# Nyström attention with a Silu feed-forward: an in-kernel list scheduler orders all engines, with DMA transposes, scores on 64x32 parts, Ln/Exp denominators, GpSimd sums and Silu

## The chip, the cores and the metric

The kernel runs on one core of one Trainium2 chip. The metric is the device time of one execution in microseconds (us), the slowest core's. Each run of a kernel is marked fast or slow. Here, with one core, slow only means more than 1.5% above the fastest run of the same kernel. PE is TensorE, PEld its weight load, DVE VectorE, ACT ScalarE, POOL GpSimd, SP SyncE.

## The reference

Eight batches of eight heads, 576 tokens of 64; then two layers on all 4608 tokens (d_model 512, d_ff 2048):

```python
q_lm = q.reshape(B, H, 32, S // 32, D).mean(axis=3)      # landmarks; k_lm the same
A, Bm, C = sm(q, k_lm), sm(q_lm, k_lm), sm(q_lm, k)      # sm: scaled scores, softmax
Z = Bm.T / (norm1(Bm) * norminf(Bm) + 1e-06)
for _ in range(6):
    Z = 2 * Z - Z @ Bm @ Z                               # Newton-Schulz
x = A @ Z @ C @ v                                        # then heads merged
h = x @ w_in
out = (h * sigmoid(h)) @ w_out
```

The kernels never form x: they make m = (Z C v) w_in for each batch, and the first layer is A times m.

## The kernel before

Its order is made by hand. The attention of batch b+1 is a generator with 26 stops. Its steps are dealt out evenly between whole units of the two layers of batch b:

```python
    def l1_unit(b, dc):
        h_ps = big("h_ps")
        for g in range(NG):
            for hf in range(2):
                mm(h_ps[:, hf, 0:HS2], m_t[b][:, g, dc * 128:(dc + 1) * 128],
                   etn_t[b][:, g, hf * HS2:(hf + 1) * HS2], start=(g == 0), stop=(g == 1))
        sig = sgp.tile([128, 2, HS2], BF, tag="sig", name="sig")
        nc.scalar.activation(out=sig, in_=h_ps[:, :, 0:HS2], func=AF.Tanh, scale=0.5)
        o = (b % 2) * S
        nc.vector.scalar_tensor_tensor(          # (tanh + 1) * h, halved in the last copy
            out=gT[:, dc, o:o + S].rearrange("p (f x) -> p f x", f=2), in0=sig, scalar=1.0,
            in1=h_ps[:, :, 0:HS2], op0=OP.add, op1=OP.mult)
    # ... cut ...
        gen = attn(b + 1) if b + 1 < B else iter(())
        NST = 26
        done = 0
        for i, u in enumerate(units):            # units: first and second layer of b
            want = (i + 1) * NST // len(units)
            while done < want:
                done += 1
                next(gen, None)
            u()
```

Transposes of q and k are VectorE's (32x32 blocks), landmark sums TensorE's (matmuls with the identity), Exp and Tanh share one table set, so ScalarE loads a table once.

The softmax here doesn't subtract the row's maximum and nothing guards it: scores larger than these inputs give would overflow.

Of the kernel before, what the change touches and what calls it, by code (L numbers as in the profile page):

```python
# [11 lines left out]
AX = mybir.AxisListType  # L12


@with_exitstack
def kernel(
# [12 lines left out]
    J = S // L  # L29
    NTOK, DMODEL = out.shape  # L30
# [4 lines left out]
    VP = VA * L  # L35
    sc = 1.0 / float(Dh) ** 0.5
    HS2 = S // 2

    constp = ctx.enter_context(tc.tile_pool(name="constp", bufs=1))
    natp = ctx.enter_context(tc.tile_pool(name="natp", bufs=2))  # L40
    vp = ctx.enter_context(tc.tile_pool(name="vp", bufs=1))
    qtp = ctx.enter_context(tc.tile_pool(name="qtp", bufs=2))
    smp = ctx.enter_context(tc.tile_pool(name="smp", bufs=2))
    stp = ctx.enter_context(tc.tile_pool(name="stp", bufs=3))
    etp = ctx.enter_context(tc.tile_pool(name="etp", bufs=2))
    mp = ctx.enter_context(tc.tile_pool(name="mp", bufs=2))
    sgp = ctx.enter_context(tc.tile_pool(name="sgp", bufs=3))
    outp = ctx.enter_context(tc.tile_pool(name="outp", bufs=3))
    bigp = ctx.enter_context(tc.tile_pool(name="bigp", bufs=2, space=bass.MemoryType.PSUM))
    opsp = ctx.enter_context(tc.tile_pool(name="opsp", bufs=2, space=bass.MemoryType.PSUM))  # L50
    smps = ctx.enter_context(tc.tile_pool(name="smps", bufs=2, space=bass.MemoryType.PSUM))

    def big(nm):
        return bigp.tile([128, 2, 512], FP, tag="big", name=nm)

    def small(nm):
        return smps.tile([128, 512], FP, tag="small", name=nm)
# [5 lines left out]

    w_in_sb = constp.tile([128, 4, DFF], BF, tag="w_in_sb", name="w_in_sb")
    w_out_sb = constp.tile([128, NDC, DMODEL], BF, tag="w_out_sb", name="w_out_sb")
    NV = 2
    vslots = [vp.tile([VP, H, 2, VI * Dh], BF, tag=f"v{i}", name=f"v{i}") for i in range(NV)]
    qk_t = [None] * B

    def load_qk(b):  # L70
        qk = natp.tile([128, 2, NG, J, Dh], BF, tag="qk", name="qk")
        for t, src in ((1, k), (0, q)):
            nc.gpsimd.dma_start(  # L73
                out=qk[:, t].rearrange("p g j d -> p g (j d)"),
                in_=src[b].rearrange("(g h) (l j) d -> (h l) g (j d)", g=NG, l=L))
        qk_t[b] = qk

    def load_v(b):
        vs = vslots[b % NV]
        for a in range(VA):  # L80
            nc.gpsimd.dma_start(
                out=vs[a * L:(a + 1) * L, :, 0, :],
                in_=v[b].rearrange("h (l a x) d -> a l h (x d)", l=L, a=VA)[a])

    def load_w_in():

        for fc in range(4):
            if fc < 2:
                nc.gpsimd.dma_start(out=w_in_sb[:, fc, :],
                                    in_=moe_w_in[fc * 128:(fc + 1) * 128, :])  # L90
            else:
                for r in range(2):
                    nc.gpsimd.dma_start(
                        out=w_in_sb[64 * r:64 * r + 64, fc, :],
                        in_=moe_w_in[fc * 128 + 64 * (1 - r):fc * 128 + 64 * (2 - r), :])

    def load_w_out():
        for c in range(4):
            nc.gpsimd.dma_start(
                out=w_out_sb[:, 4 * c:4 * c + 4, :],  # L100
                in_=moe_w_out[c * 512:(c + 1) * 512, :].rearrange("(c p) n -> p c n", p=128))

    load_qk(0)


    idb = constp.tile([128, 128], BF, tag="idb", name="idb")
    nc.vector.memset(idb, 1.0)
    nc.gpsimd.affine_select(out=idb, in_=idb, compare_op=OP.is_equal, fill=0.0, base=0,
                            pattern=[[-1, 128]], channel_multiplier=1)
    hmask = constp.tile([128, 4, L], BF, tag="hmask", name="hmask")  # L110
    nc.vector.memset(hmask, 0.0)
    for a in range(4):
        nc.vector.memset(hmask[L * a:L * (a + 1), a, :], 1.0)
    honesb = constp.tile([128, 4], BF, tag="honesb", name="honesb")
    nc.vector.tensor_copy(out=honesb, in_=hmask[:, :, 0])

    selm = constp.tile([128, NG, 2, H], BF, tag="selm", name="selm")
    nc.vector.memset(selm, 0.0)
    for g in range(NG):
        for a in range(4):  # L120
            nc.vector.memset(selm[L * a:L * (a + 1), g, :, 4 * g + a:4 * g + a + 1], 1.0)
    sel = constp.tile([2 * H, NG, 128], BF, tag="sel", name="sel")
    for g in range(NG):
        sel_ps = smps.tile([128, 1024], BF, tag="small", name="sel_ps")
        nc.tensor.transpose(out=sel_ps[0:2 * H, 0:128],
                            in_=selm[:, g].rearrange("p t h -> p (t h)"), identity=idb)
        nc.vector.tensor_copy(out=sel[:, g, :], in_=sel_ps[0:2 * H, 0:128])  # L127
    for i in range(NV):
        nc.vector.memset(vslots[i][:, :, 1, :], 1.0)

    def bc(ap, n, axis):

        shape = list(ap.shape)
        shape.insert(axis, n)
        return ap.unsqueeze(axis).to_broadcast(shape)

    etn_t = [None] * B
    m_t = [None] * B


    def attn(b):
        qk = qk_t[b]
        vs = vslots[b % NV]


        lm_ps = small("lm_ps")
        lmv = lm_ps[:, 0:256].rearrange("p (t g d) -> p t g d", t=2, g=NG)
        if b == 0:
            for t in (1, 0):
                for j in range(J):  # L150
                    mm(lmv[:, t], idb, qk[:, t, :, j, :], start=(j == 0), stop=(j == J - 1))
                yield
        else:
            for j in range(J):
                mm(lmv, idb, qk[:, :, :, j, :], start=(j == 0), stop=(j == J - 1))
                if j == 8:
                    yield
        lm = smp.tile([128, 256], BF, tag="lm", name="lm")
        nc.scalar.copy(out=lm, in_=lm_ps[:, 0:256])  # L159

        qT = qtp.tile([128, 2, NG, 2, J, L], BF, tag="qT", name="qT")


        def tp(t, g):
            if t == 0:
                nc.vector.transpose(  # L166
                    out=qT[:, 0, g].rearrange("p c j l -> p j c l"),
                    in_=qk[:, 0, g].rearrange("p j (c x) -> p j c x", c=2))
            else:
                for c in range(2):  # L170
                    nc.vector.transpose(  # L171
                        out=qT[:, 1, g, c].rearrange("p (i a) l -> p a i l", a=VA),
                        in_=qk[:, 1, g].rearrange("p (a i) (c x) -> p a i c x", a=VA, c=2)[:, :, :, c])
# [7 lines left out]
        def LB(t, g, c):  # L181
            return lmbd[:, (t * NG + g) * 2 + c].rearrange("p a l -> p (a l)")
# [311 lines left out]
```

## Time and profile before

| | before |
|---|---|
| time | 315.28 us median of 2 runs (314.69 to 315.87) |
| span, mean granted clock | 312.8 us, 0.984 |
| busy: PE, DVE, ACT, POOL | 280.7 (90%), 207.4 (66%), 166.8 (53%), 32.0 us (10%) |
| packets under 512 bytes | 944 of 18379 |

### The profile page before, as it was taken

Reading aid. Unit: us, or ns where it says so; the run is one execution under the profiler, and the core shown is the slowest. Engines: PE = TensorE matmul, PEld = TensorE weight load, DVE = VectorE, ACT = ScalarE, POOL = GpSimd, SP = SyncE. Lnnn points to the kernel's source line nnn. Section 1 sums busy time; section 2 is a strip of 40 time slices with the busy share of each in tenths; the row PEclk is TensorE's granted clock in tenths of the full one; section 3 lists DMA queues with packets and bytes.
Section 4 is the critical chain, followed back from the end, with each engine's and each line's share of the span. In section 5 each row is a group of like instructions: output and inputs, shape, how many; then the busy total and the mean of one; then the engine's idle time right before and its main releaser. Section 6 shows DMA issues by size and latency. Waiting matters only on the chain.

```text
span 312.8 us, 5645 instructions
## 1 busy us (share of the span) xinstructions
PE 280.7 (90%) x2268; PEld 161.9 (52%) x2268; DVE 207.4 (66%) x420; ACT 166.8 (53%) x277; POOL 32.0 (10%) x55
## 2 busy tenths in 40 slices
PE   0465889979999999999999999999999999999990
PEld 0443464546555654666455744665465644555440
DVE  6857689998988697579747794676448664555000
ACT  1042664775466665765475646565645757555110
POOL 7342302100210020102001020000000000000000
PEclk9998699999999999999999999999999999999997
DMA  6999999672528152193418261110111101121122
GB/s 116 210 209 207 206 210 209 86 147 69 96 50 151 56 91 56 45 161 62 83 55 145 73 90 46 52 24 16 35 55 36 44 11 45 47 47 56 52 77 75
DMA packets 18379, 28.16 MB, mean 90 GB/s; under 512 B 944, under 2 KB 9136, under 8 KB 18352
## 3 DMA queue, kind: packets, MB, share of 16 engines
q0 software_dynamic: 13600, 18.35, 34.6%
q1 hardware_dynamic: 4752, 9.44, 10.8%
q8 instruction: 18, 0.29, 0.4%
q14 instruction: 9, 0.07, 0.1%
HBM read 36.70 MB, written 9.44 MB: 147 GB/s over the span
## 4 chain that ended last, share of the span: by engine, by line
PE 72%; DVE 11%; DMA 8%; ACT 4%; issue 2%; POOL 1%; POOLq 0%; ACTq 0%
PE ops L60 36%; PE h_ps L60 18%; DVE gT L393 5%; DMA v_97<-in_v_dram 4%; PE lm_ps L60 3%; DMA w_in_sb<-in_moe_w_in_dram 3%; PE m_ps L60 3%; PE c_ps L60 2%; ACT sig L391 2%; PE w_ps L60 2%; PE sa_ps L60 2%; PE ns_ps L60 2%; DVE qT L171 2%; PE rb_ps L60 1%; ACT m L377 1%
## 5 line engine op out<-in xcount | busy, mean ns | idle before, releaser
L60 PE MATMUL ops<-w_out_sb,gT 128*128 128x512 bf16 x576 | 150.6, 379 | 0.1
L393 DVE SCALAR_TENSOR_TENSOR gT<-sig,h_ps 128x576 bf16<-128x576 bf16 x128 | 94.8, 746 | 53.2 <-ACT sig L391 53.0
L391 ACT ACTIVATE sig<-h_ps 128x576 bf16<-128x576 f32 x128 | 82.4, 651 | 56.9 <-PE h_ps L60 54.4
L60 PE MATMUL h_ps<-etn,m 128*128 128x288 bf16 x512 | 84.3, 287 | 3.4 <-DVE gT L393 2.6
L60 PEld LDWEIGHTS <-gT 128*128 128x128 bf16 x576 | 52.5, 98 | 44.3 <-issue 6.3
L60 PEld LDWEIGHTS <-m 128*128 128x128 bf16 x512 | 47.9, 98 | 34.6 <-issue 11.6
L377 ACT CAST m<-m_ps 128x1024 bf16<-128x1024 f32 x32 | 32.1, 1019 | 14.2 <-PE m_ps L60 14.1
L409 ACT ACTIVATE ost<-ops 128x512 f32<-128x512 f32 x36 | 21.4, 598 | 21.8 <-PE ops L60 21.6
L60 PE MATMUL lm_ps<-qk,idb 128*128 128x256 bf16 (+1 forms) x162 | 22.2, 289 | 6.3 <-DVE sel L127 6.3
L171 DVE STREAM_TRANSPOSE qT<-qk 128x576 bf16<-128x576 bf16 x32 | 23.8, 755 | 1.6 <-PE c_ps L60 1.6
L239 DVE SCALAR_TENSOR_TENSOR st<-st,ns_ps 128x320 bf16<-128x320 bf16 (+1 forms) x48 | 20.7, 432 | 5.5 <-PE ns_ps L60 5.4
L60 PEld LDWEIGHTS <-idb 128*128 128x128 bf16 x162 | 16.2, 112 | 11.2 <-issue 6.8
L166 DVE STREAM_TRANSPOSE qT<-qk 128x1152 bf16<-128x1152 bf16 x16 | 21.7, 1354 | 0.0
L304 ACT ACTIVATE ct<-c_ps 96x768 bf16<-96x768 f32 x16 | 12.9, 806 | 7.5 <-PE c_ps L60 7.5
L60 PE MATMUL ns_ps<-st 128*128 128x160 bf16 (+1 forms) x96 | 13.7, 223 | 2.1 <-DVE st L239 1.4
L60 PE MATMUL m_ps<-w_in_sb,zt 64*32 64x512 bf16 x256 | 13.8, 414 | 1.8 <-ACT m L377 1.0
L60 PE MATMUL c_ps<-lmbd,qT 128*96 128x128 bf16 x192 | 14.2, 219 | 0.2 <-ACT et L256 0.2
L60 PEld LDWEIGHTS <-qT 128*96 128x96 bf16 x192 | 13.3, 123 | 1.9 <-issue 0.4
L159 ACT CAST lm<-lm_ps 128x256 bf16<-128x256 f32 x8 | 3.0, 375 | 20.3 <-PE lm_ps L60 20.3
L290 DVE TENSOR_TENSOR etn<-et,rb_ps 128x576 bf16<-128x576 bf16 x16 | 12.0, 748 | 1.9 <-PE rb_ps L60 1.8
L256 ACT ACTIVATE et<-sa_ps 128x576 bf16<-128x576 f32 x16 | 10.4, 648 | 3.9 <-PE sa_ps L60 3.8
L73 POOL DMA_DIRECT2D qk<-in_k_dram x8 | 5.8, 720 | 62.3 <-PE lm_ps L60 45.4
(78 smaller groups left out, 171.4 us busy)
## 6 DMA issues: line engine op xcount, KB each, us to landing
out_dram<-ost SPq DMA_DIRECT2D x32, 256.0 KB
qk<-in_k_dram POOLq DMA_DIRECT2D x8, 576.0 KB, 5.6
qk<-in_q_dram POOLq DMA_DIRECT2D x8, 576.0 KB, 8.9
v_96<-in_v_dram POOLq DMA_DIRECT2D x12, 192.0 KB, 6.4
v_97<-in_v_dram POOLq DMA_DIRECT2D x12, 192.0 KB, 6.6
w_out_sb<-in_moe_w_out_dram POOLq DMA_DIRECT2D x4, 512.0 KB, 16.1
w_in_sb<-in_moe_w_in_dram POOLq DMA_DIRECT2D x2, 512.0 KB, 11.1
w_in_sb<-in_moe_w_in_dram POOLq DMA_DIRECT2D x4, 256.0 KB, 12.2
```

The lines of the kernel that those rows point to most:

```text
L60: nc.tensor.matmul(out=out_ap, lhsT=lhsT, rhs=rhs, start=start, stop=stop, skip_group_check=True)
L73: nc.gpsimd.dma_start(out=qk[:, t].rearrange("p g j d -> p g (j d)"), in_=src[b].rearrange("(g h) (l j) d -> (h l) g (j d)", g=NG, l=L))
L166: nc.vector.transpose(out=qT[:, 0, g].rearrange("p c j l -> p j c l"), in_=qk[:, 0, g].rearrange("p j (c x) -> p j c x", c=2))
L171: nc.vector.transpose(out=qT[:, 1, g, c].rearrange("p (i a) l -> p a i l", a=VA), in_=qk[:, 1, g].rearrange("p (a i) (c x) -> p a i c x", ...
L239: nc.vector.scalar_tensor_tensor(out=st2[:, :, lo:SW], in0=st[:, :, lo:SW], scalar=2.0, in1=ns_ps[:, 0:NG * SW].rearrange("p (g x) -> p g ...
L256: nc.scalar.activation(out=et.rearrange("p (f x) -> p f x", f=2), in_=sa[:, :, 0:HS2], func=AF.Exp, scale=sc / J)
L290: nc.vector.tensor_tensor(out=etn[:, g, :].rearrange("p (f x) -> p f x", f=2), in0=ets[g].rearrange("p (f x) -> p f x", f=2), in1=rb[:, :, ...
L304: nc.scalar.activation(out=ct.rearrange("p (f x) y -> p f (x y)", f=2), in_=c_ps[0:VP, :, 0:384], func=AF.Exp, scale=sc / J)
L377: nc.scalar.copy(out=m_sb[:, :, f * 512:(f + 1) * 512], in_=m_ps)
L391: nc.scalar.activation(out=sig, in_=h_ps[:, :, 0:HS2], func=AF.Tanh, scale=0.5)
L393: nc.vector.scalar_tensor_tensor(out=gT[:, dc, o:o + S].rearrange("p (f x) -> p f x", f=2), in0=sig, scalar=1.0, in1=h_ps[:, :, 0:HS2], op ...
L409: nc.scalar.activation(out=ost, in_=ops, func=AF.Copy, scale=0.5)
```

## The change

Its intent: give TensorE less work (scores on 64x32 parts, denominators by a block of ones, landmark sums on GpSimd), take half of VectorE's work away (Silu on ScalarE, transposes by DMA), and let a list scheduler inside the kernel place every instruction of every engine, with the Exps of a batch in one group so that Exp and Silu need few table loads. The scheduler simulates the engines with assumed durations and delays and emits the order that it finds; on the chip each engine then runs its list in order, with semaphore waits for data alone. The diff, cut to its core:

```diff
+class Plan:
+    LAG = {"PE": 0.25, "ACT": 0.22, "DVE": 0.12, "POOL": 0.2, "SP": 2.0}   # us to the next engine
+    MARGIN = 0.15                                                         # PE only
+    def run(self):
+        # ... cut: at each event each idle engine takes its ready candidate of lowest prio ...
+def act_us(n): return 0.165 + 0.000835 * n
+def dve_us(n): return 0.146 + 0.00104 * n
+def mm_us(n, count=1): return count * max(n / 2400 + 0.0025, 0.028)
 # ... cut ...
-    bigp = ctx.enter_context(tc.tile_pool(name="bigp", bufs=2, space=bass.MemoryType.PSUM))
-    opsp = ctx.enter_context(tc.tile_pool(name="opsp", bufs=2, space=bass.MemoryType.PSUM))
-    smps = ctx.enter_context(tc.tile_pool(name="smps", bufs=2, space=bass.MemoryType.PSUM))
+    pairs = [psp.tile([128, 2, 512], FP, tag=f"ps{i}", name=f"ps{i}") for i in range(4)]
+    def bank(o):
+        i = o.slot[0]
+        return pairs[i // 2][:, i % 2, :]
 # ... cut: per batch; TensorE does transposes and sums itself for the first NPE = 2 batches ...
-                nc.vector.transpose(out=qT[:, 0, g]..., in_=qk[:, 0, g]...)
+                        lambda e, t=t, g=g: nc.sync.dma_start_transpose(
+                            out=qT[:, t, g], in_=qk[:, t, g].rearrange("p j d -> p (j d)")),
-                mm(lmv, idb, qk[:, :, :, j, :], start=(j == 0), stop=(j == J - 1))
+                x = pool("la", 1152, s1, src[:, :, 0:9], src[:, :, 9:18], ...)   # GpSimd adds
+            x = A(f"Ln{g}.{b}", ..., func=AF.Ln ...)      # 1/sum = Exp(-Ln(sum))
+            x = A(f"Rs{g}.{b}", ..., func=AF.Exp, scale=-1.0 ...)
+                        func=AF.Exp, scale=sc / J, accum_out=csum[...]           # C's sums
+                cts[g] = [A(f"ct{g}.{b}", [("SP", 0.9)], lambda e, ce=ce, ct=ct:
+                            nc.sync.dma_start_transpose(
+                                out=ct, in_=ce.rearrange("p i x -> p (i x)")), ...)]
-        nc.scalar.activation(out=sig, in_=h_ps[:, :, 0:HS2], func=AF.Tanh, scale=0.5)
-        nc.vector.scalar_tensor_tensor(...)
+                                   out=gm[:, dc, :], in_=bank(cell["o"]), func=AF.Silu),
 # ... cut ...
+    order = P.run()
+        for o, e, t, end, switch in order:
+            o.emit(e)
```

## The prediction

> **What bounds the kernel now.** I read the page's busy shares first, then the stretches of the span, then the chain that ended last, then the groups of instructions, and last the timeline at the start.
>
> ```profile
> PE 280.7 (90%) x2268; PEld 161.9 (52%) x2268; DVE 207.4 (66%) x420; ACT 166.8 (53%) x277; POOL 32.0 (10%) x55
> ...
> PE   0465889979999999999999999999999999999990
> ```
> ```profile
> 20.00:30.00 10.00, 5.87 (x80) 4.01 (x88) 6.92 (x21) 2.65 (x7) 2.99 (x4) 0.97 1.14 206
> 30.00:60.00 30.00, 26.04 (x254) 16.12 (x238) 26.09 (x52) 17.20 (x28) 6.30 (x10) 0.89 1.12 193
> 140.00:180.00 40.00, 39.90 (x352) 23.60 (x350) 29.08 (x59) 24.14 (x42) 3.14 (x5) 1.00 0.41 83
> ```
> PE is busy 90% of the span, and in the middle 39.9 of 40 us at full clock. The loss is at the start: PE does little before 35 us, and from 30 to 60 us DVE is as busy as PE. The columns after the length are PE, PEld, DVE, ACT, POOL, the granted clock, DMA and GB/s.
>
> A busy PE may still be waiting inside its pipeline, so I take what a matmul costs from unbroken runs in the chain:
> ```profile
> 141.39 0.67 PE c_ps L60 x12
> 144.04 1.11 PE w_ps L60 x24
> 227.84 0.98 PE h_ps L60 x8
> 230.94 0.98 PE lm_ps L60 x9
> 287.29 18.14 PE ops L60 x84
> 305.50 0.60 ACT ost L409
> ```
> That is 216 ns for a 512-column matmul (18.14/84), 122 ns for 288 columns, 109 for 256, 56 for 128 and 46 for w_ps, whose pairs lie side by side. From the timeline:
> ```profile
> 23.14 0.39 PE L60 MATMUL cs_ps<-honesb,et 128*128 128x4 bf16 x10
> 152.73 1.67 PE L60 MATMUL ops<-w_out_sb,gT 128*128 128x512 bf16 x7
> 154.33 0.41 PE L60 MATMUL m_ps<-w_in_sb,zt 64*32 64x512 bf16 x8
> 154.68 0.39 PE L60 MATMUL ops<-w_out_sb,gT 128*128 128x512 bf16 x1
> ```
> Ten weight loads with tiny matmuls start about 25 ns apart ((0.39 - 0.165 of one)/9). Eight matmuls on 64x32 parts of 512 columns hold PE 0.35 us together (154.33 to 154.68), and the seven full ones before them took 1.60 instead of 1.51 us, so going into the parts costs some 0.09 us more.
>
> **PE's work before**, count by spacing, us: second layer 576 x 0.216 = 124.4; first layer 512 x 0.1225 = 62.7; landmark sums 126 x 0.109 and 36 cold ones = 17.6; C scores 192 x 0.056 = 10.8; A scores 64 x 0.122 = 7.8; softmax sums, transposes and broadcast 2.0 + 2.2 + 3.9 = 8.1; w_ps 192 x 0.046 = 8.9; m_ps 32 x 0.44 = 14; Newton steps 6; the rest 2. Sum 262. The last matmul starts near 305, so 43 us are idle or waiting: 25 before 35 us (some 10 us of work in there) and 18 after.
>
> **What the Trainium skill says.** "TensorE: Matmul & The Clock Gate", Back-to-back issue gap: N/2.4 + 2.5 ns warm. The trace agrees: 216 ns at 512. So the two layers, 187 us, can't shrink by re-cutting 288 columns into 512 and 64. "ScalarE: Activation LUTs", What ACT_TABLE_LOAD costs: about 1283 ns for each change of table set, and a drain. The trace has one load, 1283 ns; the new kernel's ACT list has 15 of them. "GPSIMD Engine Reference", 2.1 Instruction dispatch: two inputs cost about 2.5 cycles an element on that engine at 1.2 GHz, some 2.1 ns; no such instruction ran before. "DMA: Bandwidth & Descriptors", Latency and other measured facts: 261 GB/s effective for a DMA transpose; this trace has none either.
>
> **The change, part by part.** The built order gives the counts.
>
> (1) *DVE freed.* Before:
> ```profile
> L393 DVE SCALAR_TENSOR_TENSOR gT<-sig,h_ps 128x576 bf16<-128x576 bf16 x128 | 94.8, 746 | 53.2 <-ACT sig L391 53.0
> L391 ACT ACTIVATE sig<-h_ps 128x576 bf16<-128x576 f32 x128 | 82.4, 651 | 56.9 <-PE h_ps L60 54.4
> L171 DVE STREAM_TRANSPOSE qT<-qk 128x576 bf16<-128x576 bf16 x32 | 23.8, 755 | 1.6 <-PE c_ps L60 1.6
> L166 DVE STREAM_TRANSPOSE qT<-qk 128x1152 bf16<-128x1152 bf16 x16 | 21.7, 1354 | 0.0
> ```
> Silu on ACT replaces Tanh and the DVE product, which takes 94.8 us off DVE; DMA transposes (PE transposes with copies for batches 0 and 1) take 45.5 us off. DVE gets most m, lmT and ost copies in return, about 5 us a batch, 40 us. DVE goes from 207 to near 110 us. It was nearly the bound only from 30 to 60 us, so most of this lies beside PE's work; what counts is that a first-layer buffer comes free after one ACT instruction instead of ACT and then DVE (0.65 + 0.75 us), and that the Newton chain stops queueing behind gT.
>
> (2) *ACT.* Per batch 18 Silus of 0.60 (ost, 128x512, took 598 ns) = 10.8; exps, Ln and reciprocal exps of C and A about 5.8; pb 0.2; two table loads 2.6; three or four copies 2.4. Sum near 22 us against 28 to 29 us of PE per batch: below PE, but no Silu runs inside the Exp group of some 9 us. PE must then live on second-layer work (4.5 chunks x 3.46 = 15.5 us per batch), and the order puts it there, four matmuls after each Newton step.
>
> (3) *PE.* Layers unchanged: 124.4 and 256 x 0.216 + 256 x 0.029 = 62.7. C and A scores: 32 groups of eight on 64x32 parts; 288 columns are 93 ns shorter than the 0.35 us group, so 0.25 each plus entries, 1.3 per batch = 10.4 instead of 18.6. Denominators by a block of ones: 32 x 0.122 = 3.9 instead of 8.1. Landmark sums go to GpSimd except in batches 0 and 1; with those batches' transposes PE keeps 72 cold x 0.107 + 72 x 0.056 = 11.7, against 17.6. Landmark transposes 1.8, C transposes 1.3, C times v 8 x 1.15 = 9.2, m 13.4, Newton 6, small scores 3, rest 1.8. Sum 250: 12 to 13 us less.
>
> (4) *Start.* Before, the memsets of v and sel held the landmark sums to 12.5 us although k had landed at 6.9; pb began at 18.2 and the first m_ps at 29.8, 11.5 us later. Now PE begins at about 7; with q down near 9.9 and the copies shared by ACT and DVE, pb comes near 15.7 after a table load. The same chain of 11 us gives m at 26.5 to 27. But ACT's list has all of batch 1's Exp group before the first Silu: m copies to 29.5, then pb, C, A, copies, Ln, exps of about 6.5 us and waits, then a load. First Silu near 38.5, against the first Tanh at 36.1. It looks like no gain, but batch 1's attention is then done too: 25 us of PE's 250 are behind it, so 13.5 us idle instead of 25.
>
> (5) *From there.* 225 us of PE work are left at 38.5. The first layer of batch 0 is bound by ACT (18 Silus and copies of m for batch 1, 13 us, against 9 of PE): 4.5 us lost. The steady part I charge 3%, some 5 us. The order leaves 212 second-layer matmuls (46 us) with nothing between them for the end, which run at full rate. PE ends at 38.5 + 225 + 4.5 + 5 = 273; before, the end came 7.4 us after PE (312.8 - 305.4). Span 280; the timed run is 2.5 above the span (315.3 against 312.8), so 282.
>
> **Rivals.** (a) *The fixed order meets late inputs.* PE runs in a fixed list; where a ct transpose through DMA lands late, or a DVE Newton step slips, PE stands still with other work behind it. A transpose of 128x768 bf16 is 197 KB, 0.8 us at the skill's rate (an estimate), plus the start-up that loads show as some 2 us. If it takes 5 us rather than 3, two waits of 1 to 2 us in each of six batches add 10 to 20 us: 292 to 302. For it: the DMA figures are unmeasured here. Against: the DMA share is down to 0.41 by 140 us.
> (b) *GpSimd too slow or in DVE's way.* Per batch 2 x 2304 elements at 2.1 ns plus overhead is 11 us, hidden in 28 us; only batch 2 is tight, as its q and k land at 45 to 50 us, after w_out. If DVE instructions wait for it, the Newton chain stretches, and 5 to 10 us come on top: 287 to 292.
> (c) *ACT becomes the bound.* Its 22 us per batch with table loads and waits could reach PE's 28; then 290. The fixed order speaks against: copies went to DVE.
> (d) *Nothing is lost.* If PE keeps its work dense from 36 on, 272.
>
> **Range and chances.** The arithmetic of work removed is firm (12 us); the start and waits are worth 20 us and could fail by half, or succeed by 10 more. 269 to 296 covers (b), (c), (d) and the milder half of (a). Only (a) at its worst and (b) together undo the gain. Faster by over 2% 0.96, within 2% 0.03, slower 0.01.
>
> **What would show it.** First Silu at 37 to 40 us. PE matmul count near 2,200 and eight-part groups of scores at 0.25 us. DVE busy under 125 us, ACT 170 to 195. About 40 to 50 us of pure second layer at the end. PE idle in the middle under 5%, waits of PE on ct or on lm from POOL under 1 us each. Wrong if C times v waits for transposes by over 1 us each time, if the first Silu is past 44 us, or if ACT passes 85% busy in the middle.

## More of the kernel before

The columns are the length, then PE, PEld, DVE, ACT and POOL busy (with instructions), the granted TensorE clock, the DMA share and GB/s:

```profile
0.00:35.00 35.00, 16.16 (x175) 11.16 (x176) 26.15 (x60) 9.55 (x15) 15.92 (x30) 0.92 1.05 188
35.00:70.00 35.00, 30.20 (x269) 18.71 (x268) 31.19 (x63) 20.96 (x37) 4.93 (x8) 0.98 0.98 170
70.00:260.00 190.00, 188.95 (x1581) 108.74 (x1579) 135.07 (x278) 115.86 (x195) 11.15 (x18) 1.00 0.33 67
```

From 70 to 260 us TensorE is idle for 1.05 us of 190. Whatever the change does there, it can't make TensorE denser; it can only give it less to do.

## The result, and the profile after

The time after is 365.27 us, median of 2 runs (364.79 to 365.75), against 315.28: the ratio is 1.159 (95% interval 1.153 to 1.165). Ratios here and below are the mean time of one kernel's fast runs over that of the other's in the same rounds, so not quite the ratio of the medians. The prediction, 282 us with 269 to 296, was wrong in direction.

The busy rows of the changed kernel's page, its TensorE row and its clock row in 40 slices of 9.1 us, and the chain's shares by engine:

```profile
PE 278.2 (76%) x2216; PEld 131.9 (36%) x2216; DVE 116.0 (32%) x272; ACT 186.6 (51%) x371; POOL 105.8 (29%) x121
...
PE   2586967883398788796889996989598998888860
...
PEclk9969555999599989999899999899899999999995
...
PE 50%; ACT 17%; DVE 13%; DMA 11%; issue 5%; ACTq 0%; DVEq 0%; POOLq 0%
```

No engine is full, and TensorE holds half of the chain that ended last. Its dense row of nines is gone, and so is its full clock. The stretches, cut as before:

```profile
0.00:35.00 35.00, 20.34 (x272) 16.51 (x273) 15.24 (x44) 17.54 (x39) 20.16 (x35) 0.90 1.09 183
35.00:70.00 35.00, 26.11 (x212) 11.24 (x204) 17.56 (x33) 22.17 (x48) 17.38 (x19) 0.61 1.21 189
70.00:260.00 190.00, 150.72 (x1281) 67.84 (x1279) 73.90 (x176) 113.76 (x227) 68.30 (x68) 0.95 0.66 104
```

These give an account of the 51 us between the two spans (364.0 and 312.8):

- *Idle TensorE.* 364.0 - 278.2 = 85.8 us against 312.8 - 280.7 = 32.1: 54 us more. Up to 70 us both kernels idle 23.6 us. From 70 to 260 us it is 39.3 against 1.05 us; eight gaps of over 1 us make 24.8 of the 39.3, and 54 shorter ones 14.5. After 260 us it is 22.9 (104.0 less 81.1 busy) against 7.4.
- *Clock.* If each stretch's busy time is multiplied by its granted clock, TensorE did some 254 us of full-speed work in 278 busy us (from 260 us on it is 36.84 us at 0.96 and 44.23 at 0.94). Before it is 278 in 281 (from 260 us on 40.00 at 1.00 and 5.42 at 0.87). So the lower clock costs some 20 us more. This is an estimate, as the clock is a mean over the stretch and not over its busy time.
- *Work.* The same products say that TensorE has some 24 us less to do, more than the 12 that I had worked out.

The work removed is real; idle time and a colder clock took it back three times over. What TensorE waited for, in the view of waits (total us, times, longest us):

```profile
PE ps L309 <- DMA ct<-ce: 20.0, 4, 11.4
...
PE ps L309 <- ACT ost L319: 8.8, 13, 0.7
...
PE ps L309 <- DVE st L577: 5.7, 8, 1.9
```

ct is the transposed C that a DMA makes for C times v. In the chain that ended last (start, us, what):

```profile
82.21 14.73 DMA ct<-ce
...
253.25 7.32 DMA ct<-ce
```

And SyncE's own queue (SPq), which issues the transposes and the stores:

```profile
45.97 34.56 SPq L456 DMA_TRANSPOSE qT<-qk  x8
81.41 0.71 SPq L820 DMA_DIRECT2D out_dram<-ost  x1
82.21 8.07 SPq L670 DMA_TRANSPOSE ct<-ce  x2
```

Eight transposes of q and k held that queue for 34.6 us. The twelve C transposes by DMA (768 packets of 256 bytes each) show how much their time varies with what moves beside them. "Landing" is here and below the last update of the transpose's semaphore, for which the engines wait. The four with next to nothing beside them (issued at 152.65, 154.01, 191.25 and 192.60) land 2.75 to 2.80 us after their issue begins; the packets of the first run 1.10 us. The four beside output stores alone land after 3.6 to 7.3 us, among them the one of 253.25 in the chain. The four beside loads land after 5.5 to 14.7 us; the one issued at 82.21 has 1,179 KB of loads and 262 KB of stores beside it.

At the end, 208 second-layer matmuls with nothing else between them (the plan has 212) take 55.5 us (297.25 to 352.75); at the 216 ns of the kernel before they would take 45:

```profile
330.30 0.59 ACT L319 COPY ost<-ps 128x512 f32<-128x512 f32 x1 [6.34 <-PE ps L309]
...
330.94 1.02 PE L309 MATMUL ps<-w_out_sb,gm 128*128 128x512 bf16 x4 [0.72 <-ACT ost L319]
...
332.04 0.58 ACT L319 COPY ost<-ps 128x512 f32<-128x512 f32 x1 [1.16 <-PE ps L309]
332.68 6.20 PE L309 MATMUL ps<-w_out_sb,gm 128*128 128x512 bf16 x28 [0.72 <-ACT ost L319]
```

The two second-layer banks are halves of one PSUM tile, and waits are kept by tile. The built program makes the copy out of one half wait for matmuls into the other, and the next four matmuls wait for that copy. TensorE stops 0.72 us twice per pair of chunks.

The first Silu comes at 51.25 us (predicted 38.5), m starts at 34.1 us (26.5 to 27). Groups of VectorE and GpSimd (count, busy, mean ns):

```profile
L620 DVE TENSOR_TENSOR etn<-et,ln 128x576 bf16<-128x576 bf16 x16 | 17.2, 1074 | 1.4 <-ACT ln L614 1.4
...
L707 DVE SCALAR_TENSOR_TENSOR qbd<-st,pbs,hmask 128x128 bf16<-128x128 bf16 x16 | 11.1, 733 | 0.3
...
L486 POOL TENSOR_TENSOR sa<-qk 128x1152 f32<-128x1152 bf16 x12 | 28.8, 2397 | 0.9
```

Before, etn took 748 ns and qbd 347. The Trainium skill, "SBUF — State Buffer", Who interferes with whom, says that a VectorE instruction with two SBUF inputs contends with a GpSimd instruction that reads SBUF, and that the port pair which they share is an exclusive lock. The trace agrees: the longest qbd is 2.5 us and the longest bm (64 elements, 224 ns before) 2.39 us, as long as the GpSimd sum of 2.40 us (1152 elements at 2.08 ns each, as the prediction took them).

### The profile page after: what moved, and what is told of

The parts are those of the page before. It is cut to its first block, busy times and chain, and to the rows that moved or that the text cites. A ratio compares the mean times of both kernels' runs of the same rounds, so it can differ in the third digit from the quotient of the medians.

```text
span 364.0 us, 5602 instructions
## 1 busy us (share of the span) xinstructions
PE 278.2 (76%) x2216; PEld 131.9 (36%) x2216; DVE 116.0 (32%) x272; ACT 186.6 (51%) x371; POOL 105.8 (29%) x121
## 4 chain that ended last, share of the span: by engine, by line
PE 50%; ACT 17%; DVE 13%; DMA 11%; issue 5%; ACTq 0%; DVEq 0%; POOLq 0%
PE ps L309 50%; DMA ct<-ce 9%; ACT gm L761 6%; ACT m L319 4%; DVE m L321 3%; ACT ost L319 2%; DVE st L577 2%; DMA qk<-in_k_dram 2%; DVE qbd L707 1%; DVE ost L321 1%; DVE qT L321 1%; ACT qT L319 1%; DVE bm L536 1%; DVE etn L620 1%; ACT L875 1%
## 5 line engine op out<-in xcount | busy, mean ns | idle before, releaser
L309 PE MATMUL ps<-w_out_sb,gm 128*128 128x512 bf16 x512 | 129.1, 390 | 8.2 <-ACT ost L319 6.7
L309 PE MATMUL ps<-etn,m 128*128 128x64 bf16 (+1 forms) x512 | 82.4, 298 | 13.5 <-ACT gm L761 5.1
L761 ACT ACTIVATE gm<-ps 128x512 bf16<-128x512 f32 x128 | 69.5, 600 | 30.3 <-PE ps L309 26.8
L309 PEld LDWEIGHTS <-gm 128*128 128x128 bf16 x512 | 48.1, 99 | 65.9 <-issue 19.0
L577 DVE SCALAR_TENSOR_TENSOR st<-st,ps 128x320 bf16<-128x320 bf16 (+1 forms) x48 | 21.2, 442 | 65.1 <-PE ps L309 60.7
L486 POOL TENSOR_TENSOR sa<-qk 128x1152 f32<-128x1152 bf16 x12 | 28.8, 2397 | 0.9
L321 DVE CAST m<-ps 128x512 bf16<-128x512 f32 x32 | 21.0, 688 | 23.8 <-PE ps L309 12.0
L319 ACT CAST m<-ps 128x512 bf16<-128x512 f32 x32 | 18.3, 587 | 8.9 <-DVE m L321 7.0
L486 POOL TENSOR_TENSOR sb<-sa 128x512 f32<-128x512 f32 (+1 forms) x24 | 22.2, 925 | 1.4
L620 DVE TENSOR_TENSOR etn<-et,ln 128x576 bf16<-128x576 bf16 x16 | 17.2, 1074 | 1.4 <-ACT ln L614 1.4
L643 ACT ACTIVATE ce<-ps 128x288 bf16<-128x288 f32 x32 | 12.7, 412 | 7.7 <-PE ps L309 7.7
L611 ACT ACTIVATE ln<-ps 128x576 f32<-128x576 f32 x16 | 10.5, 654 | 11.5 <-PE ps L309 11.5
## 6 DMA issues: line engine op xcount, KB each, us to landing
qk<-in_k_dram POOLq DMA_DIRECT2D x8, 576.0 KB, 10.7
w_in_sb<-in_moe_w_in_dram POOLq DMA_DIRECT2D x4, 256.0 KB, 10.7
```

Of the source, the lines that this page charges most:

```text
L309: nc.tensor.matmul(out=out_ap, lhsT=lhsT, rhs=rhs, start=start, stop=stop, skip_group_check=True)
L319: nc.scalar.copy(out=out, in_=in_)
L321: nc.vector.tensor_copy(out=out, in_=in_)
L486: lambda e: nc.gpsimd.tensor_tensor(out=o_, in0=a_, in1=b_, op=OP.add),
L577: nc.vector.scalar_tensor_tensor(out=s2[:, :, lo:SW], in0=s[:, :, lo:SW], scalar=2.0, in1=ps[:, 0:NG * SW].rearrange("p (g x) -> p g x", g ...
L611: x = A(f"Ln{g}.{b}", [("ACT", act_us(S))], lambda e, g=g, ln=ln: nc.scalar.activation(out=ln, in_=pair(me[f"S{g}"])[:, :, 0:HS], func=AF. ...
```

## The experiments

The theory after reading the trace: TensorE's list is fixed, and was planned with delays shorter than the chip's (whether they are, see e16). TensorE stands wherever something is late, and the late things are (T1) DMA transposes beside loads, (T2) copies that share a PSUM tile, (T3) VectorE behind GpSimd, (T4) everything else by some tenths. Rivals: one of these alone explains it; or the start alone does; or the freed VectorE was on the path and something else ate a gain. Eighteen kernels ran, all with correct results. The variants are the changed kernel with switches; with all switches as in the change the order is the same. Each switch makes the scheduler plan anew, so a variant differs from its parent in its whole order, and a difference of a few us may be the new order's; no run separates the two. The kernel before ran in the same rounds: 314.9 to 316.3 us by its medians. An experiment's lines number differently, as switches add lines. With only one fast run there is no ratio. The spread given is that of all runs of a kernel, slower ones too, unless "fast runs" is said; the profiles of e1, e7, e9, e12, e13, e16 and e17 are of slower runs.

**e1: banks of their own.**

```diff
-    pairs = [psp.tile([128, 2, 512], FP, ...) for i in range(4)]
+    pairs = [psp.tile([128, 2, 512], FP, ...) for i in range(2)]
+    ones = [psp.tile([128, 512], FP, ...) for i in range(4)]      # banks 4 to 7
```

> The changed kernel with one edit: accumulator banks 4 to 7 are single-bank tiles of their own, where the changed kernel has four tiles of two banks each (so two-bank results may use two pairs, not three). Theory A, that waits are tracked by tile and so a copy out of one bank waits for matmuls into its neighbour and the other way round: the last stretch of pure second layer (212 matmuls) shrinks from 57 us to 47 to 49, PE's waits on ost copies (8.8 and 1.9 us) go to under 2 us, PE no longer waits for Silus in pairs, and the whole comes to 328 to 345 us. Rival B, that late DMA transposes and the slow start make nearly all of the loss: the tail shrinks at most a little and the whole stays at 355 to 365.

Measured: one fast run of 350.0 us, three of 360.0 to 361.6. The tail's stops are gone, as one line of its timeline shows:

```profile
330.68 12.29 PE L315 MATMUL pone<-w_out_sb,gm 128*128 128x512 bf16 x56
```

That is 56 matmuls in one run, at 219 ns each. But TensorE's waits on ct grew from 20.0 to 36.3 us (25.5 and 10.8 in two rows), the longest from 11.4 to 18.0. (The profile is of one of the slower runs.) Theory A's tail came true (204 matmuls in 44.3 us), its time of 328 to 345 us did not. T2 is real in the tail, but part of what it frees is spent on the next late transpose. It brings 15 us by the one fast run and 5 by the medians. The granted clocks of fast and slower runs hardly differ (0.886 to 0.896), so I take their distance for a matter of when transposes and loads meet; that is argued, not shown.

**e2, e3, e4: parts of the change put back on TensorE.** In the change TensorE does the C transposes, the q and k transposes and the landmark sums itself for the first two batches only:

```diff
-        on_pe = b < NPE                                  # NPE = 2, for all three
+        qt_pe, ct_pe, sum_pe = b < QT_PE, b < CT_PE, b < SUM_PE
+        # e2: CT_PE = 8   e3: SUM_PE = 8   e4: all three 8
```

> The changed kernel with the transposes of the exponentials of C (ct) done by PE and copies in all eight batches, as batches 0 and 1 have it; q and k still go through DMA transposes and the landmark sums stay on GpSimd. Theory B, late ct landings stop PE in its fixed order: PE's 20 us of waits on ct go away, PE gets about 4 us of work more, the whole comes to 338 to 350 us. Rival A (shared two-bank tiles make the loss, the ct wait would be filled with other waits): 358 to 368.

> The changed kernel with the landmark sums done by PE in all eight batches; the transposes stay with DMA in batches 2 to 7. Theory C, GpSimd's sums hold up DVE's instructions with two operands in SBUF: etn falls from 1074 ns mean to about 750, qbd from 733 to about 350, bm from 536 to about 225, and although PE has 12 us more to do the whole comes to 350 to 362. If those DVE delays cost nothing on the path, the whole rises by the work, to 370 to 378.

> The changed kernel with all transposes and all landmark sums on PE in all eight batches: no DMA transpose and no GpSimd sum. PE gets about 29 us more to do (54 more 128-column matmuls x 6 batches for q and k, 12 for C, 36 for the sums, with weight loads), and 14 more copies per batch go to ACT and DVE. If B and C together make the loss: 335 to 350 us, no wait for DMA after 50 us, DVE means as before the change. If A and the start make it: 370 to 395, the work added on top.

| | time, us | ratio to before | what the trace shows |
|---|---|---|---|
| e2, C transposes | 349.6 (347.0 to 351.7) | 1.103 (1.097 to 1.109) | no wait on a DMA of ct, but 3.9 us on its copies; PE on output copies 9.0, on ln 7.4; an output tile waits 8.2 us for its store |
| e3, landmark sums | 377.7 (372.6 to 380.7; fast 372.6 and 377.2) | 1.186 (1.176 to 1.197) | etn 753, qbd 349, bm 225 ns, as before; PE on ct 21.6 us |
| e4, all three | 367.0 (365.3 to 367.8) | 1.161 (1.155 to 1.165) | etn 750 ns; no wait on a DMA transpose; PE on the copies of its own q and k transposes 11.5, on output copies 9.0, on gm 7.1 us |

e2 brings 16 us for 5 us of added TensorE work (by the plan): of the parts taken singly, T1 is the largest loss. e3 shows T3's mechanism (with no GpSimd sum VectorE's means are those of before) and that it is not what TensorE waits for first: the time grew by 10 us by the fast runs and 12 by the medians, about the 12 us of added matmuls. e4 adds some 29 us of planned TensorE work and costs 2 us: so some 27 us of TensorE's time had been lost to the DMA transposes and to GpSimd's sums, and to the colder clock that went with them (0.910 in the changed kernel, 0.951 in e4). e4 doesn't tell these apart.

**e5: e1 and e2 together.**

> The C transposes on TensorE in all batches, and the four PSUM banks that the two layers use made tiles of their own. Theory (late C transposes and the copies' shared tiles are two separate losses): the changed kernel's 365.3 us, less about 16 us as in the run with the C transposes on TensorE alone (349.5), less about 9 us for the tail's waits on the output copies: 338 to 344 us; the waits of TensorE on the output copies fall from 9 us to under 2. Rival (TensorE's fixed order only moves the loss to the next late input): 346 us or more, with a wait of another name grown by what the copies' waits lost.

Measured: one fast run of 325.5 us, the others 332.6 to 335.6. No wait on a DMA of ct, and none on an output copy among the listed ones. By the fast runs that is 40 us under the changed kernel, where the parts alone gave 15 and 16 (by the medians 32, and 5 and 16). Together they seem to give more than their sum, as in e1 time won in one place was lost at the next late transpose; with one fast run each in e1 and e5, the size of that is uncertain. In 70 to 260 us TensorE is now busy 169.0 of 190 us.

**e6: loads planned after the C transposes.**

```diff
-            load_qk(b, 100.0 * b - 150, dk)
+            load_qk(b, 100.0 * b - 150, dk + [last[b - 1]["ct1"]])     # load_v too
```

> All of the change kept, and the loads of a batch's q, k and v held until the C transposes of the batch before have landed, so that no load runs beside a C transpose. Theory (the loads' traffic slows the transposes): each C transpose of batches 2 to 7 lands within 3.5 us of its issue, TensorE's waits on them fall from 20 us (with 21 us of the weight loads') to under 5, and the time falls to 345 to 355 us. Rival (the transposes of q and k ahead in the same queue, or the output stores, make them late): some C transposes still take 5 us or more and TensorE still waits on them for 12 us or more, and the time stays within 5 us of 365.

Measured: 351.1 us (348.8 to 352.5), ratio 1.113 (1.108 to 1.119). The waits on ct fell from 20.0 to 14.4 us, the longest from 11.4 to 5.0. The C transposes land in 2.8 to 9.2 us. The time fell into the theory's range, but not by its mechanism: "within 3.5 us" failed, and the waits on ct give 5.6 of the 14 us. Where the rest comes from is not shown. That transposes still came late is in part an error of mine in the experiment: the scheduler's dependency sets the load's place in GpSimd's list and makes no wait on the chip. When transposes slip, loads still run beside them. And loads are not all: the one issued at 225.45, when GpSimd had issued its last load long before, had 262 KB of other traffic beside it, all of it stores, and took 6.3 us to land.

**e7: e5, and the eighth Silu of batch 0 before batch 1's Exp group.**

```diff
-            [me["sb"]], p0 + 12, table="exp", group=grp)
+            [me["sb"]] + ([gm_ops[0][7]] if b == 1 else []), p0 + 12, table="exp", group=grp)
```

> The run with the C transposes on TensorE and the split banks, and batch 1's Exp group made to wait for the eighth Silu of batch 0. Theory (the first layer waits for batch 1's Exp group, and those 13 us are lost on TensorE): the first Silu comes at 36 to 40 us instead of 49 to 51, and the time is 6 to 12 us below that of the run without it. Rival (TensorE has enough other work then, or only has its idle time later, when batch 1's attention is late): the first Silu is as early, but the time is within 3 us.

Measured: one fast run of 322.7, others 331.5 to 333.3; against e5, 2 to 3 us, which is within what runs of one kernel differ by here. The first Silu came at 36.1 us, 13.7 us earlier than in e5. The rival is right: the start's order moves idle time, it doesn't make it. From 51 to 70 us the clock is 0.53, and batch 1 is late instead.

**e8: the q and k transposes on TensorE, the C transposes by DMA.** (QT_PE = 8.)

> The transposes of q and k on TensorE in all batches (some 13 us of added matmuls by the plan, and their copies), the C transposes left to the DMA. Theory (loads slow the C transposes): the C transposes are still late where loads run, TensorE still waits on them for 10 us or more, and the time is 365 to 378 us. Rival (the queue of 24 transposes of q and k is what makes them late): all C transposes land within 3.5 us, their waits fall under 5 us, and the time is 350 to 362 us in spite of the added work.

Measured: 364.3 us (362.8 to 365.7), ratio 1.156. The waits on ct fell to 3.6 us, and all C transposes landed in 2.7 to 6.1 us. That looks like the rival, that the 24 transposes of q and k make the C transposes late. But the loads had moved too: here at most 419 KB of them ran beside a C transpose, where it was up to 1,179 KB in the changed kernel. So e8 can't tell the q and k transposes from the loads. The rival's waits (under 5 us) came true, its 3.5 us for each transpose and its time did not. The added work took the gain back.

**e9: e5, with GpSimd's sums cut.** The sum of 1152 elements became six of 192, that of 512 two of 256.

> The run with the C transposes on TensorE and the split banks (325 to 335 us, with one run in four at the low end), and GpSimd's sum of 1152 elements cut into six of 192 and that of 512 into two. Theory (a VectorE instruction that reads two operands from SBUF is held for as long as the GpSimd instruction beside it lasts, and TensorE in its fixed order waits behind it): the longest such VectorE instruction falls from 3.1 us to under 1.2, TensorE's waits on qbd and bbd (4.0 and 3.7 us) halve, and the time falls by 3 to 8 us. Rival (the two share the port access by access, or these waits are hidden): the mean of the etn products stays at 1.0 us or more, and the time is within 2 us.

Measured: fast runs 328.5, 330.4 and 330.4 us, ratio 1.043; two others near 337. The mechanism is confirmed: qbd fell from 783 to 440 ns on average and from 2.5 to 0.64 us at its longest, TensorE's wait on it from 4.0 to 0.3 us. (The "3.1 us" in the expectation was two instructions; the longest single one was 2.6.) The time did not fall, because of one new stop:

```profile
113.47 23.99 SPq L470 DMA_TRANSPOSE qT<-qk  x4
...
131.14 0.59 ACT L333 COPY ost<-pone 128x512 f32<-128x512 f32 x1 [24.88 <-DMA out_dram<-ost]
...
131.78 0.58 PE L323 MATMUL pone<-w_out_sb,gm 128*128 128x512 bf16 x1 [24.09 <-ACT ost L333]
```

Four q and k transposes hold the queue for 24 us (and four more did from 86.0 to 110.2). A store issued at 110.24 lands at 131.07, 20.8 us later. ScalarE stands for want of an output tile, and TensorE stops for 24 us. (This profile is of one of the two slower runs; e10's is of a fast one and has a stop of 20 us of the same kind.) After it the clock is cold:

```profile
131.00:134.00 3.00, 2.00 (x7) 0.96 (x7) 0.00 (x0) 1.14 (x2) 0.00 (x0) 0.50 1.23 184
134.00:137.00 3.00, 3.00 (x24) 1.61 (x23) 0.95 (x4) 1.53 (x3) 1.52 (x3) 0.73 1.25 155
```

The Trainium skill, "TensorE: Matmul & The Clock Gate", What's actually happening, says that the array falls to half rate after about 3.4 us of idling and returns after about as long a busy stretch. The trace agrees: 0.50, then 0.73, then 1.00 from 137 us.

**e10: e9, planned with longer delays.**

```diff
-    LAG = {"PE": 0.25, "ACT": 0.22, "DVE": 0.12, "POOL": 0.2, "SP": 2.0}
+    LAG = {"PE": 0.45, "ACT": 0.42, "DVE": 0.32, "POOL": 0.4, "SP": 2.0}
```

> The run before it, with the scheduler told that each result reaches the next engine 0.2 us later than it assumed (PE 0.45 instead of 0.25, ACT 0.42, DVE 0.32, POOL 0.4). Its own planned end grows from 282 to 290 us. Theory (TensorE's fixed order leaves too little other work between steps that depend on one another, as it was planned with delays shorter than the chip's): TensorE is busy 93% or more between 70 and 260 us instead of 89%, and the time falls by 4 to 12 us. Rival (the lost time is not in those steps): the time grows by 3 to 10 us, as the plan does.

Measured: fast runs 326.7 and 327.6, ratio 1.035, two others near 336. Against e9 some 3 us. The stop is still there (an output tile waits 20.3 us for its store), and hides the rest. Outside it TensorE is denser: from 120 to 260 us it is busy 132.2 of 140 us, in e5 129.1. Not decisive alone; e16 and e17 answer it.

**e11: Silu alone, in the kernel before.**

```diff
-        nc.scalar.activation(out=sig, in_=h_ps[:, :, 0:HS2], func=AF.Tanh, scale=0.5)
-        nc.vector.scalar_tensor_tensor(out=gT[...], in0=sig, scalar=1.0, in1=h_ps[...], ...)
+        nc.scalar.activation(out=gT[...], in_=h_ps[:, :, 0:HS2], func=AF.Silu)
```

> The kernel before in its own order, with the one operation of the change that frees VectorE most: Silu on ScalarE in place of Tanh and VectorE's product (128 products, 103 us of VectorE's 207). Theory (VectorE's time lies beside TensorE's, and Silu costs a table load of 1.28 us at each change from Exp to Silu and back, which in this order is up to ten per batch): VectorE's busy time falls to some 100 to 115 us, ScalarE gets 50 to 75 more table loads, and the time grows to 325 to 350 us. Rival (VectorE was on the path): the time falls below 310 us.

Measured: 330.2 us (329.2 to 333.1), ratio 1.046 (1.040 to 1.053). Its busy row:

```profile
PE 283.6 (87%) x2233; PEld 163.9 (50%) x2268; DVE 122.1 (37%) x292; ACT 236.0 (72%) x334; POOL 32.0 (10%) x55
```

VectorE gave up 85 us and the kernel got slower. ScalarE had 58 table loads of 1283 ns, 74 us, in the same edit, so e11 alone doesn't show that VectorE was off the path. From 70 to 260 us TensorE's 1.05 us of idle time in the kernel before shows it. (The 103 us of the expectation are 94.8.) The table loads are why a change to Silu needs the Exps grouped, and with that the new order.

**e12, e13, e14: what stops TensorE for 24 us?** All from e9: stores issued by ScalarE; six output tiles instead of three; the q and k transposes on TensorE too, so that no DMA transpose is left.

```diff
-        nc.sync.dma_start(out=out[...], ...)             # e12: nc.scalar.dma_start
-    ost_r = ring(outp, [128, DMODEL], FP, "ost", 3)      # e13: 6
                                                          # e14: QT_PE = 8
```

> The run with the split banks, the C transposes on TensorE and the cut sums (328.5 to 330.4 us in its fast runs), with the output stores issued by ScalarE, so that they no longer stand behind the q and k transposes in SyncE's queue. Theory (those transposes hold the queue for up to 24 us, the stores behind them hold the output tiles, and TensorE stops for up to 24 us): ScalarE's and VectorE's waits for an output tile's store fall from 27 us to under 3, the single stop of 24 us goes, and the time is 303 to 313 us. Rival (the stores are late as the DMA engines are full, not the queue): the stop stays over 10 us and the time over 322.

> The same run with the stores left on SyncE and six output tiles in place of three. Theory as above: a stop of 24 us is covered but for some microseconds by three more tiles of some 6 to 8 us each: 305 to 316 us. Rival (the q and k of the next batch come as late as the stores, and TensorE waits for them instead): the stop moves to a wait on qT of over 10 us and the time stays over 322.

> The same run with three output tiles and the transposes of q and k on TensorE too, so that no DMA transpose is left. The plan has 12.5 us more TensorE work (271.1 against 258.6). Theory: no stop, no wait for a store over 3 us, and the time is 24 us less and 12.5 to 15 us more than the fast 328.5 to 330.4: 313 to 323 us. Rival (the stop had another cause): 335 us or more.

e12: fast runs 334.9 and 339.9 us (others 344.3 and 349.3), ratio 1.068. e13: fast runs 323.0 and 327.4 (others 330.9 and 337.2), ratio 1.029 (1.020 to 1.039), so slower or not at 2% is unclear. e14: 342.0 us (341.4 to 342.8), ratio 1.083. The three theories' numbers failed, and the traces (of slower runs in e12 and e13) say why. In e12 and e13 TensorE no longer waits for an output tile; it waits for the landmark sums of the next batch, 13.9 us in e12, and in e13:

```profile
PE ps L325 <- POOL lm L502: 18.3, 1, 18.3
```

GpSimd itself waited up to 21.6 (e12) and 27.7 us (e13) for a q and k transpose to leave the buffer that its next load writes. So neither the queue nor the tiles were the root: the slow transposes were, and each cure moved the stop to the next thing that waits for them. In e14 there is no stop (no gap of TensorE over 2.4 us from 70 to 260 us). What is left there are 81 gaps of 20.9 us together; the kernel before has 16 gaps of 1.0 us.

**e15: e9, loads of q, k and v planned away from the transposes.**

> The run with split banks, C transposes on TensorE and cut sums (fast runs 328.5 to 330.4 us), with the loads of a batch's q and k held until the q and k transposes of the batch before have landed, and the loads of its v until its own have: no load of q, k or v runs beside a DMA transpose. Theory (transposes beside loads take 4 to 9 us each instead of 1.1 to 1.5, and the stop of 14 to 24 us comes from that): from 100 us on each of the q and k transposes lands within 4 us of its issue, the four of a batch hold the queue under 8 us, no wait of TensorE is over 4 us, and the time is 303 to 315 us. Rival (the transposes are slow beside anything, stores too): they still take over 10 us for four, a stop of over 10 us stays, and the time is over 322.

Measured: 324.0 us (323.3 to 324.5), ratio 1.026. The theory's numbers failed and the rival's came true: a stop of 13.1 us is left, and the time is over 322. But the experiment did not do what the text says. As in e6, the scheduler only held the load's place in GpSimd's list:

```profile
85.11 24.78 SPq L472 DMA_TRANSPOSE qT<-qk  x4
...
90.15 0.73 POOL L369 DMA_DIRECT2D qk<-in_k_dram  x1
```

Loads were issued at 90.15, in the midst of four transposes that then held the queue for 24.8 us. Batch 2's four transposes did run apart from loads, but for the end of one; they landed in 3.3 to 3.9 us, where without the hold (e9) the first two took 16.0 and 17.7 us. So apart they are quick; I did not manage to keep them apart.

**e16: e14 with the longer delays of e10.**

> The run with no DMA transpose (342.0 us, TensorE busy 89% between 70 and 260 us in 81 gaps of 20.9 us), with the scheduler told of delays longer by 0.2 us. Its planned end grows from 296 to 300 us. Theory (without the transposes what is left is that each result comes some tenths later than planned, and TensorE, whose order is fixed, waits each time): TensorE's gaps there fall from 20.9 to under 12 us, and the time falls by 4 to 12 us, to 330 to 338. Rival (the gaps have another cause): they stay within 3 us of 20.9, and the time grows by some 4 us as the plan does.

Measured: three fast runs, 326.6 to 327.7 us, ratio 1.037, so 15 us under e14, more than expected. So the same operations, planned with results 0.2 us later, end sooner although the plan ends 4 us later. The profiled run fell at a granted clock of 0.567 and took 473.4 us, so its gaps can't be compared. e18 has the longer delays too, and no DMA transpose before 153.61 us; so its trace (second line) can stand beside that of e14 (first line) up to 150 us:

```profile
70.00:150.00 80.00, 69.26 (x634) 34.85 (x644) 35.34 (x78) 56.94 (x116) 54.08 (x91) 1.00 0.46 85
...
70.00:150.00 80.00, 73.12 (x665) 36.93 (x676) 38.08 (x86) 56.83 (x117) 44.69 (x75) 0.98 0.47 87
```

TensorE's idle time there falls from 10.7 to 6.9 us. That more room in the plan helps is shown. That the chip's delays are longer than the planned ones is not: in the changed kernel, an engine that waited for one of TensorE, ScalarE and VectorE began 33 to 53 ns (medians by pair of engines; the ends of matmuls are modelled) after the end of what it waited for, while the plan assumed 120 to 250 ns. So the room probably covers what the plan doesn't have at all, such as late transfers, a cold clock and VectorE behind GpSimd; that is argued, and no run divides it among these.

**e17: the longer delays alone, in the changed kernel.**

> The changed kernel with one thing changed: the scheduler is told that results reach the next engine 0.2 us later (PE 0.45 instead of 0.25, ACT 0.42, DVE 0.32, POOL 0.4; what it assumes of transfers is as it was). Its planned end grows from 276.6 to 281.5 us. Theory (a good part of the loss is the fixed order's short delays, the rest the DMA transposes): 345 to 358 us, with TensorE's waits on the C transposes still over 8 us. Rival (the short delays only matter once the transposes are gone): 360 us or more.

Measured: one fast run of 349.4 us, the others 354.8 to 359.7 (365 without). TensorE waits on ct for 24.4 us. By the fast run it is 16 us, by the medians 9: too little room in the plan is part of the loss, and the DMA transposes keep theirs.

**e18: e16, with DMA transposes for the last two batches.** (QT_PE = CT_PE = 6.)

> The run with no DMA transpose and longer delays (327 us in its fast runs), with the DMA transposes put back for the last two batches alone, where all loads but those of v are done. TensorE's planned work falls from 270.1 to 265.1 us, the planned end from 300.4 to 296.2. Theory (a DMA transpose costs nothing where no load runs beside it): each of those transposes lands within 4 us, TensorE never waits over 2 us for one, and the time is 320 to 326 us. Rival (stores and v loads are enough to make them late): a wait of over 4 us on them, and 328 us or more.

Measured: 320.8 us median (318.6 to 321.7), ratio 1.013 (1.008 to 1.019). The middle of the span:

```profile
70.00:260.00 190.00, 178.52 (x1615) 88.14 (x1644) 86.18 (x208) 141.43 (x284) 70.60 (x117) 0.99 0.47 82
```

TensorE never waits for a transpose among the listed waits. But the mark "within 4 us" failed for q and k: 4.2 to 10.6 us, beside v loads and stores, while the C transposes took 2.8 to 3.5. No listed wait of TensorE came of it; that the plan had room for it is argued. This is the best version found: 44 us under the changed kernel, within 2% of the kernel before and still 4 to 5 us over it. No version beat the kernel before.

## Why the prediction was wrong, point by point

**(1) VectorE freed: right.** 116.0 us (predicted near 110, under 125), and beside TensorE's path, as the 1.05 us of idle time before shows. I left out that GpSimd would lengthen VectorE's two-operand instructions (e3, e9). Rival (b) names it and sizes it at 5 to 10 us; its own effect could not be isolated, as another stop took its place in e9.

**(2) ScalarE: right.** 186.6 us, 51%, against 170 to 195. Mis-sized inside: the 32 accumulator reads of C's sums cost 209 ns each, 6.7 us that I had not counted.

**(3) TensorE's work: right in direction, and small in size.** 2216 matmuls (near 2,200 predicted), and 16 parts of the scores in 0.47 us at 18.05 us. The busy time of 278 us against my 250 is the clock: at full speed it's some 254 us (the estimate above).

**(4) The start: failed.** The step "First Silu near 38.5" was 12.7 us off, and "13.5 us idle instead of 25" was 23.6 us up to 70 us in both kernels. The 25 was too high to begin with: before 35 us TensorE was busy for 16.2 us at a clock of 0.92, so it idled 18.8. The "25 us of PE's 250" were done at the first Silu (32.1 busy us at a clock of 0.78, some 25 at full speed, an estimate), but at 51.25 instead of 38.5. pb came at 17.8 instead of 15.7. "The same chain of 11 us" took 16 us to m: TensorE's list has batch 1's transposes between batch 0's Newton steps, and stood for their copies out of PSUM, as three lines of the timeline show:

```profile
29.32 0.72 PE L309 MATMUL ps<-idb,qk 128*128 128x128 bf16 x10 [0.73 <-ACT qT L319]
...
32.71 0.27 PE L309 MATMUL ps<-qbd,wsb 128*128 128x128 bf16 x2 [0.73 <-DVE qT L321]
...
51.25 1.08 ACT L761 ACTIVATE gm<-ps 128x512 bf16<-128x512 f32 x2
```

The first two lines each stand 0.73 us for a copy of batch 1's q or k, the second of them just ahead of batch 0's last product before m; the third is the first Silu. The clock was 0.61 from 35 to 70 us. e7 shows that repairing the Silu's place alone brings only 2 to 3 us.

**(5) "The steady part I charge 3%, some 5 us": the step that failed most.** Idle time from 70 to 260 us is 39.3 us where I had 9.5 (5 and 4.5). I took before's density for granted in a kernel whose order is made in another way. The hand-made order puts a whole unit between dependent steps; the scheduler puts what its assumed delays ask for, and not more. What the runs showed in its place: late C transposes (e2, 16 us), too little room in the plan (e16, 15 us without DMA transposes; e17, 9 to 16 us with them), and stops that move from one late input to the next (e9, e12, e13, e15). Two of the prediction's own marks of being wrong came true with it: waits of C times v on transposes (20.0 us in four), and a first Silu past 44 us. "At full rate" for the tail failed too, by 10 us: halves of one PSUM tile (e1, and a tail without those stops in every version with split banks).

**Rival (a) had the mechanism; its size failed.** I set a transpose at 0.8 us plus some 2 us of start-up. Alone it was just that, 1.10 us of packets and 2.8 us to landing. "If it takes 5 us rather than 3, two waits of 1 to 2 us" was the mis-sized term: beside loads a C transpose took up to 14.7 us to land, beside stores alone up to 7.3, and waits reached 11.4 us. My argument against, the DMA share of 0.41 in the kernel before, was read from a kernel without these transposes. With them the share from 70 to 260 us is 0.66; it was 0.33 before, and is 0.31 in e14, which has none. And giving a 0.96 chance of faster rested on a sum of removed work, when the thing that made the old kernel dense was being replaced.

What stays open: how much of the 21 us of clock is a loss of its own and how much follows from the stops; why a DMA transpose slows by that much beside loads or stores, and not only by its share; how much the q and k transposes add to that; what the room in the plan covers; and the last 4 to 5 us of e18.

## What to carry to other kernels

A fixed order is only as good as the times it was planned with: compare the plan's times with the trace, and leave room in the plan, since 0.2 us added per result (the one value tried) made a longer plan and a kernel shorter by 15 us without DMA transposes, and by 9 to 16 with them. When an engine that was 99% dense loses work and gets a new order, the density is the first thing to defend, not the work. In this kernel DMA transposes were quick where next to nothing ran beside them, neither loads nor stores, and a cure must go to the late transfer itself: freeing the queue, the tiles or the banks one at a time only moved the wait, and a planned order is no wait on the chip.

## What the Trainium skill lacked or had wrong

- "DMA: Bandwidth & Descriptors", Latency and other measured facts, gives 261 GB/s for a DMA transpose; the page has no figure for one beside other traffic, nor for a store issued behind transposes. Here the packets of a 197 KB transpose alone ran 1.10 us (179 GB/s) and it landed after 2.8 us; one beside 1,179 KB of loads and 262 KB of stores landed after 14.7 us; four 295 KB ones held the issuing queue for 24 us, and a store issued behind four such landed after 20.8 us.
- "ScalarE: Activation LUTs": it names the accumulator output without its cost. Here each use added an instruction of 209 ns (32 of them).
- "TensorE: Matmul & The Clock Gate": it gives no share of busy time at which a TensorE with many short gaps loses its clock. In the changed kernel 26.1 of 35 us busy (35 to 70 us) went with a clock of 0.61.
